# Attention front of a fused kernel: scale in the cast, negated maxima, constants made on chip, new order

## The chip, the cores and the metric

The kernel runs on one core of one Trainium2 chip. The metric is device time in microseconds (us), the median of several runs; lower is better. A core has a matrix engine (PE, with its weight loads shown as PEld), a vector engine (DVE), a scalar engine (ACT), a general engine (POOL), and a queue that issues DMAs (SP). ACT and POOL can issue DMAs too. Engines run their own instruction lists in order and wait for each other by semaphores.

## What is computed

Windowed attention with four sink tokens, then a feed-forward layer with a sigmoid-gated unit.

```python
def _attn_ref(q, k, v, n_sink, window):     # q, k, v: (4, 8, 768, 64)
    scale = 1.0 / np.sqrt(D)
    scores = scale * np.matmul(q, k.transpose(0, 1, 3, 2))
    keep = is_sink | in_window              # first 4 keys, or the last 128
    scores = np.where(keep, scores, -1000000000.0)
    scores = scores - np.max(scores, axis=-1, keepdims=True)
    a = np.exp(scores)
    a = a / (np.sum(a, axis=-1, keepdims=True) + 1e-09)
    return np.matmul(a, v).astype(np.float32)

def _moe_ref(x, w_in, w_out):               # x: (3072, 512), d_ff 2048
    h = x @ w_in
    g = h * (1.0 / (1.0 + np.exp(-1.702 * h)))
    return (g @ w_out).astype(np.float32)
```

## The kernel before

**Tiling.** The 4 x 768 rows are 24 blocks of 128 queries. Blocks 0, 6, 12, 18 are the first of each batch: they see only their own 128 keys. Every other block sees its own keys, the block's before it, and the four sinks. The first four are done first, then the rest in order (`BLOCKS`). The feed-forward works on groups of blocks: 0, 6, then 12 and 18 together, then pairs.

**One block, by the names of its operations** (b is the block; _0 and _1 are halves of four heads):

- `q`b, `k`b, `v`b: loads with a cast to 16 bits, issued by POOL. `wi0..3`, `wo0..3`: quarters of w_in and w_out, also by POOL.
- `tq`, `tk` and `cq`, `ck`: transposes of queries and keys on PE for the first blocks, and the copy out of PSUM (ACT or DVE). Later blocks use a DMA transpose (`tqk`, SP).
- `msk` (first blocks only): the causal mask is added into the scores by a matmul of an identity (`identb`) with a table (`bias0`). `sc`: the scores.
- `ks`b: sink keys of a batch packed into `ksb` (zeroed by `zk`), by two small copies. `snk`: sink scores. `ms`: their maximum. In block 1 it adds `bias1`, a 4-column mask.
- `pk`: copies masked scores in place, by the table `later`. `mx`: row maximum. First blocks: `nb` (maximum times -scale), then `bx`, the exponential with scale and that bias. Other blocks: `sb`, `ssb` (subtract), then `ex`, `exs`.
- `ta`, `ca` (PE transpose, copy) or `tat` (DMA transpose): probabilities transposed. `sp`, `so`: POOL cuts them into the previous block's part and the own part.
- `av`: probabilities times values, with the sinks' values from `vsb`. `nm`: normalization. `tx`, `cx` or `txd`: the result transposed.
- `h`g_u: first feed-forward product of group g. `th` and `g`: the gate. `o`b_n: second product. `ev`, `st`: copy out of PSUM and store.

**Sink values.** `zs` sets `vsa` to one, `vsa0..3` load four value rows of each batch into it (SP), and `vsb0..3` multiply that by the table `own` into `vsb`.

**Constants.** Six tables lie in the program and are loaded: `ident`, `identb`, `later`, `bias0` (32 KB each), `own` (32.5 KB) and `bias1` (1 KB). `za0..3`, `zv`, `z1`, `zk`, `zs` are memsets on DVE.

**Order.** All operations are listed in a plan, and a written list (`ORDER`, lines 55 to 89) names them by number in the order in which they are emitted; a letter picks the engine where there is a choice (d DVE, a ACT, p POOL, s SP). Each engine executes its own in that order. PSUM has three buffers `mm` for transposes and feed-forward products, two `sc`, one `av`; a new use waits until an older user has let its buffer go.

The front, decoded, engine by engine (before):

```
PE   tq0 msk0 tk0 sc0 tk18 tq12 tk6 tk2 ta0_0 tq6 msk6 ta0_1 tk12 av0_0 sc6 tk1 av0_1 tq1 tq18 tx0 snk1 ta6_0
     h0_1 av6_0 ta6_1 msk12 sc12 av6_1 h0_3 tx6 h0_2 h1_3 h1_2 msk18 h1_1 sc18 h0_0 ta12_0 h1_0 ta12_1 av12_0 o0_0
     ta18_0 av12_1 o0_1 sc1 tx12 o6_0 av18_0 tq2 o6_1 snk2 ta18_1 o6_2 o0_2 ta1_1 av18_1 o6_3 sc2 tx18 ta1_0 o0_3
     tk4 tq4 tk3 tq3 h2_2 ...
DVE  zs zk zv za1 z1 ck0 mx0_0 za0 vsb0 nb0_0 mx0_1 vsb2 nb0_1 ck6 vsb1 ks0 ck2 za2 ks6 za3 nm0_0 mx6_0 mx6_1 ...
ACT  ident own identb bias0 cq0 ck18 bx0_0 cq12 bx0_1 cq6 ca0_0 ca0_1 ck12 ck1 cq1 bx6_0 cx0 bx6_1 cq18 th0_1 ...
POOL q0 k0 k18 q12 k6 k2 q6 vsb3 v0 k12 v6 q18 k1 q1 wi1 wi3 wi2 v12 wi0 wo0 wo1 q2 v18 wo2 wo3 k3 q4 k4 q3 q5 v2
     v1 k5 sp1_1 v7 k7 sp1_0 so1_0 so1_1 v5 v4 k8 v3 q7 sp2_0 so2_0 q8 sp2_1 so2_1 ...
SP   vsa3 vsa1 vsa0 later vsa2 bias1 st0_ tqk5 tat3 tqk7 ...
```

Of the kernel before, what the change touches and what calls it, by code (L numbers as in the profile page):

```python
# [11 lines left out]
FP32 = mybir.dt.float32  # L12
FP16 = mybir.dt.float16
# [27 lines left out]
LH = 1.0  # L41
HW = set()
LD4 = 0.65
LD, LW, QKX, ATX, XTX, STX, SPX2 = 0.97, 2.55, 1.55, 1.56, 0.77, 0.85, 1.9
AHEAD = 4
TQ = set(BLOCKS[:8])
# [5 lines left out]
RING = dict(RING,qkn=7)  # L52


ORDER = """
1a 9 6 8d 100 15 4a 5a 11 14 7 96 0a 23 94 21 3s 98 17 2s 29 18 104 107 105a 101p 102 103d 16 108 171 20 109 150 19
172a 10 95d 125 110 24 112 225 111 99d 26 151a 113 126d 27 114 115 97d 88 127 106 128a 130 92 226d 116a 117 12 90 129
148 118a 119 13 131 149a 22 120 194 132 121 86 196 195a 135 173 197a 87 133 122 134 89 123 199 124a 200 138 30 136 613
139d 137 25 152 142 174a 140 143 153 614 141d 615 154 91 144 155 619 156 145 157 158 146 616 93 620 147d 159 160 621
637 32 617 634 638 618 176 639 635 631 36 175 636 177 632 610 178 633 161 611 181 35 628 162a 179 612 180 163 182 165  # L60
622 164d 166 629 184 183 33 167 623 185d 168 39 198 630 169 31 204 640 170a 205 188 227 189 641 228a 201 28 230 186
206 642 231 209 202 624 187a 203 215 190 38 643 208 191 207 229 216d 210 644a 192 217 235 211 43 193a 625 232 212a 236
41 280 282 626a 256 281d 258 213 283a 627 233 652 259a 214 237 257a 649 653 218 238 234 261 661 241 40 650 262 654 239
285 37 260 651 662 242 286 304 44 655 266 243a 263 34 219 656 646 663 42 657 658 647 244 220 664 648 659 245 267 670
45 665 660 240 221 671 264 268 246 672 247a 269 265 248 667 222 270 249 666 250 284 668 271 251 48 676 669 46 290 252
323 673 47 253 287 677 291 254 306 272 678 288 255a 674a 223 292 679 273 224a 293 289 682 680d 294 51 307 305 683 50
688 295 308 311 49 686 309 675 52 684 687 312 689 692 310 685 313 276 693 690 314 277 296 315 704 297 344 324 345 705
327 691 316 53 330 325 694 326 361 331 274 695 696 275 328 698 697 681 332 278 317 699 279a 333 329 298 334 318 343
299 700 346 54 347 300 706 55 349 335 701 57 301 350 302 645 319 303a 707 348 702a 352 351 716 708a 320 353 362 336
321 717 354 720 322 337 365 724 709 59 721 363 399 714 364 368 60 712 715 703 369 725 722 366 713 340 355 723 710 341  # L70
367 718 711 356 371 370 338 719 732 64 339 372 726 342 56 733 62 382 381 373 61 383 727 387 384 359 734 360 385 728
388 401 735 390 386 729 374 419 389 750 402 391 375 730d 400 736d 751 748 392 67 406 403 742 66 404 752 65 743 407 749
740 63 753 378 738 379 408 376 739 744 377 393 409 357 405 745 746 358 741 394 420 380 747 439 58 410 754 440 423 421
760 422 426 397 755 427 411 398 761 424 457 756 425 762 428 757 429 430 412 766 758d 438 759 413 767 763 431 444 69
441 770 737 442 71 768 771 445 72 764a 772 769 446 68 416 443 773 780 432 447 417 788 781 433 448 414 774 415 73 458
459 789 775 460 449 464 395 778 396 461 776 418 779 465 782 777 462 436 495 450 783 463 466 790 75 765 437 731 784 467
74 468 434 451 785 435 476 791 482 786d 800 792a 479 454 793 801 798 469 455 794 514 452 795 802 453 808 803 456 477
804 809 478 470 799 483 796 480 471 806 797 485 805 484 816 76 481 810 77 486 474 80 496 475 817 70 502 807 499 487
497 82 811 498 78 500 818 503 81 516 822 504 819 823 505 517 501 812 820a 506 515 821 824 488 518 813 489 825 507 828
814d 83 472 826 552 473 79 519 832 827 521 829 535 836 833 536 522 492 837 834 508 523 830 524 493 509 520 844 831 84  # L80
835 490 534 525 491 845 540 494 541 838 537 846 526 542 839 538 512 787 847 513 543 840 539 544 553 852 848a 545 527
573 864 853 574 590 528 510 841 511 865 559 860 842d 529 546 861 556 862 530 850 547 554 854 851 555 85 560 531 855
856 532 557 858 533 857 561 866 859 558 550 815 562 591 563 551 872 597 867 863 592 564 873 593 598 868 843 594 548
849 880 595 869 596 881 600 565 888 599 549 874 889 870d 566 601 886 875 884 876a 602 567 885 572 568 878 877 575 569
879 892 570 578 882 571 893 603 576 887 890 579 604 894 891 577 883 900 580 581 895 582 901 607 912 608 583 896 913
605 871 897 606 902 898a 910 584 916 911 585 914 917 918 915 908 919 906 909 586 907 903 587 922 588 920 589 923 609
921 904a 928 924 929 925 930 926d 946 931 947 934 942 935 932a 948 943 933 940 905 927 936 941 899 938 937 949 944 939
956 945 950 957 951 958 952 962 953 963 954a 959 964 955 960d 965 961 966d 967
# [48 lines left out]
def _consts():  # L137
    j = np.arange(P)[None, :]
    p = np.arange(P)[:, None]
    later = j > p  # L140
    bias0 = np.where(later & (j >= 4), NEG, 0.0).astype(ml_dtypes.bfloat16)
    bias1 = np.where(later[:, :4], NEG, 0.0).astype(ml_dtypes.bfloat16)
# [3 lines left out]
    return (  # L146
        np.eye(P, dtype=np.float16),
        later.astype(np.uint16),
        bias0,
        bias1,  # L150
        own.reshape(32, 8 * D1),
    )
# [3 lines left out]
def kernel(  # L156
# [20 lines left out]
    ident_np, later_np, bias0_np, bias1_np, own_np = _consts()  # L177
    ident_d = nc.inline_tensor(ident_np, name="cident")
    identb_d = nc.inline_tensor(ident_np.astype(ml_dtypes.bfloat16), name="cidentb")
    later_d = nc.inline_tensor(later_np, name="clater")  # L180
    bias0_d = nc.inline_tensor(bias0_np, name="cbias0")
    bias1_d = nc.inline_tensor(bias1_np, name="cbias1")
# [37 lines left out]
    o_bias0 = cdma("bias0", bias0, bias0_d.ap(), -1000)  # L220
    o_ident = cdma("ident", ident, ident_d.ap(), -999)
    o_bias1 = cdma("bias1", bias1, bias1_d.ap(), -998)
    o_later = cdma("later", later, later_d.ap(), -997)
    o_own = cdma("own", ownm, own_d.ap(), -996)
    o_identb = cdma("identb", identb, identb_d.ap(), -999.5)
# [111 lines left out]
    for bb in range(Bsz):  # L337
        o = plan.add(
            f"vsa{bb}", SP, 0.75, lambda bb=bb: nc.sync.dma_start(vsa[:, bb, 0:D], v[bb, :, 0:4, :]),
            deps=[z_s], dma=("v", 0.3), key=-500 + bb,  # L340
        )

        def vs_build(e, bb=bb):
            (nc.vector if e == DVE else nc.gpsimd).tensor_tensor(
                out=vsb[0:32, bb].rearrange("p l (j d) -> p (l j) d", d=D1),
                in0=vsa[:, bb].unsqueeze(1).to_broadcast((32, 8, D1)),
                in1=ownm.rearrange("p (n d) -> p n d", d=D1),
                op=ALU.mult,
            )

        o_vsb.append(plan.add(f"vsb{bb}", {DVE: 0.6, POOL: 1.15}, 0, vs_build, deps=[o, o_own, z_v], key=20))
# [12 lines left out]
    for pos, b in enumerate(BLOCKS):  # L364
# [5 lines left out]
        qkb = qkT[:, SLOT[b]]  # L370


        buf, n, unit = tunit[b]
        if b in OCT:
            parts = []
            before = used_slot.pop(SLOT[b], [])
            for w in (1, 0):
                tp = ps("mm", (P, 8, 4, 16), FP32, f"t{'qk'[w]}{b}")

                def t_qk(w=w, buf=buf, n=n, tp=tp):  # L380
                    for t in range(8):
                        for l in range(2):
# [11 lines left out]
                        f"c{'qk'[w]}{b}", {DVE: 0.6, ACT: 0.5}, 0,  # L394
                        lambda e, w=w, tp=tp, qkb=qkb: copy(
                            e, qkb[:, 4 * w : 4 * w + 4].rearrange("p c (u t) -> p c u t", t=8),
                            tp().rearrange("p t c u -> p c u t"),
# [5 lines left out]
        elif b in TQ:  # L403
# [3 lines left out]
            for w in (1, 0):  # L407

                def t_qk(w=w, buf=buf, n=n, tp=tp):
                    src = buf()[:, n, w].rearrange("p h d -> p (h d)")  # L410
                    for c in range(4):
# [9 lines left out]
                        lambda e, w=w, tp=tp, qkb=qkb: copy(e, qkb[:, 4 * w : 4 * w + 4], tp()[:, 4 * w : 4 * w + 4]),  # L421
# [19 lines left out]
        if r == 0:  # L441

            def sink_keys(bb=bb, qkb=qkb):
                for hl in range(2):
                    rows = slice(64 * hl, 64 * hl + 64)
                    nc.vector.tensor_copy(
                        out=ksb[rows, bb, :, 4 * hl : 4 * hl + 4], in_=qkb[rows, 4:8, 0:4]
                    )

            o_ks[bb] = plan.add(f"ks{b}", DVE, 0.45, sink_keys, deps=o_qkt[b] + [z_k], key=K0 - 10)  # L450
# [79 lines left out]
        for hf in range(2):  # L530
# [12 lines left out]
            def rowmax(hf=hf, t=sc[hf], own=own, small=small, ms=ms):  # L543
                part = small[:, 4 * hf : 4 * hf + 4].rearrange("p (j l) -> p l j", l=2)
                nc.vector.tensor_reduce(out=part, in_=t()[:, :, :, own], axis=AX.X, op=ALU.max)  # L545
# [353 lines left out]
```

## Time and profile before

| | |
|---|---|
| median of 3 runs | 233.18 us (233.18 to 233.24) |
| the profiled execution | 232.43 us, of which the span of instructions 230.7 us |
| granted PE clock | 1.00 |
| PE busy | 217.0 us, 94% of the span, 2202 matmuls |
| DVE busy | 154.5 us, 67% |
| ACT busy | 139.8 us, 61% |
| POOL busy | 111.2 us, 48% |
| moved by DMA | 32.07 MB, mean 139 GB/s |
| loads of q, k, v | 24 each, 128 KB as written, median 5.4 to 5.7 us from issue to landing |
| w_in, w_out | 4 loads each, 512 KB, median 10.4 and 15.4 us |

The span runs from the first to the last instruction; the profiled execution's own time has 1.7 us around it. In the profile an engine's line gives its busy share in forty equal slices, in tenths. The timeline lists instructions with their start and length in us and, in brackets, how long the engine had been idle before and what it had waited for. Matmuls are pipelined, so a busy PE can hide short stalls. A landing time is the issue's start plus the time to landing.

### The profile page before, as it was taken

Reading aid. Unit: us, or ns where it says so; the run is one execution under the profiler, and the core shown is the slowest. Engines: PE = TensorE matmul, PEld = TensorE weight load, DVE = VectorE, ACT = ScalarE, POOL = GpSimd, SP = SyncE. Lnnn points to the kernel's source line nnn. Section 1 sums busy time; section 2 is a strip of 40 time slices with the busy share of each in tenths; the row PEclk is TensorE's granted clock in tenths of the full one; section 3 lists DMA queues with packets and bytes.
Section 4 is the critical chain, followed back from the end, with each engine's and each line's share of the span. In section 5 each row is a group of like instructions: output and inputs, shape, how many; then the busy total and the mean of one; then the engine's idle time right before and its main releaser. Section 6 shows DMA issues by size and latency. Waiting matters only on the chain. (4 is left out here: it accounts for less than half of the span.)

```text
span 230.7 us, 5431 instructions
## 1 busy us (share of the span) xinstructions
PE 217.0 (94%) x2202; PEld 151.6 (66%) x2202; DVE 154.5 (67%) x388; ACT 139.8 (61%) x220; POOL 111.2 (48%) x129
## 2 busy tenths in 40 slices
PE   0878899999999999999999999999999999999994
PEld 0666865876586686486577496486686686775863
DVE  2487899999979976987797848668577847121001
ACT  2278774874597687168378386786358486631531
POOL 8983435995393869077392619265350312300000
PEclk9999999999999999999999999999999999999999
DMA  5999999999999899999999989999647542402312
GB/s 76 167 189 200 206 198 180 168 134 91 153 182 168 159 242 131 148 162 135 165 196 136 196 172 131 131 185 110 140 92 114 142 99 45 99 0 45 114 71 91
DMA packets 120904, 32.07 MB, mean 139 GB/s; under 512 B 112016, under 2 KB 117936, under 8 KB 120880
## 3 DMA queue, kind: packets, MB, share of 16 engines
q0 software_dynamic: 69888, 13.64, 72.2%
q1 hardware_dynamic: 50512, 17.96, 38.7%
q8 instruction: 17, 0.28, 0.5%
q10 hardware_dynamic: 480, 0.13, 0.3%
q14 instruction: 7, 0.06, 0.1%
HBM read 27.46 MB, written 6.29 MB: 146 GB/s over the span
## 5 line engine op out<-in xcount | busy, mean ns | idle before, releaser
L786 PE MATMUL hT<-xT,w_in 128*128 128x256 f16 (+1 forms) x832 | 93.2, 264 | 1.5 <-ACT gT L816 0.5
L836 PE MATMUL o<-w_out,gT 128*128 128x512 f16 (+2 forms) x400 | 92.1, 371 | 0.0
L786 PEld LDWEIGHTS <-w_in 128*128 128x128 f16 x832 | 73.9, 98 | 14.1 <-issue 3.7
L816 ACT ACTIVATE gT<-hT 128x512 f16<-128x512 f32 x80 | 45.8, 597 | 33.1 <-PE hT L786 32.9
L836 PEld LDWEIGHTS <-gT 128*128 128x128 f16 x400 | 36.1, 98 | 33.3 <-issue 1.9
L637 POOL TENSOR_SCALAR_AFFINE_SELECT atp<-at 128x1024 f16<-128x1024 f16 (+1 forms) x22 | 22.3, 1015 | 72.9 <-DMA at<-a 69.9
L545 DVE TENSOR_REDUCE mx<-sc 128x4 f32<-128x512 f32 x48 | 32.7, 683 | 0.8 <-PE sc L478 0.5
L606 ACT ACTIVATE a<-e 128x1056 f16<-128x1056 f32 (+2 forms) x24 | 22.5, 938 | 15.4 <-issue 12.5
L535 DVE COPY_PREDICATED sc<-later,sc 128x512 f32<-128x512 uint16 x40 | 26.8, 689 | 3.6 <-PE sc L483 3.3
L582 DVE TENSOR_TENSOR e<-sc,mx 128x512 f32<-128x512 f32 x40 | 26.7, 684 | 0.7
L722 DVE RECIPROCAL rcp<-av 128x4 f32<-128x4 f32 x48 | 8.6, 179 | 24.0 <-PE av L712 22.1
L637 POOL TENSOR_SCALAR_AFFINE_SELECT at<-at 128x1024 f16<-128x1024 f16 (+1 forms) x22 | 22.2, 1009 | 1.4
L271 POOL DMA_DIRECT2D v<-in_v_dram x24 | 21.7, 906 | 2.0 <-DMA w_in<-in_moe_w_in_dram 1.2
L723 DVE TENSOR_TENSOR xn<-av,rcp 128x256 f16<-128x256 f32 x48 | 20.4, 424 | 1.7
L241 DVE COPY osb<-o 128x512 f32<-128x512 f32 (+2 forms) x10 | 6.3, 634 | 21.2 <-PE o L836 21.1
L606 ACT ACT_TABLE_LOAD x12 | 15.4, 1283 | 6.1 <-DVE e L596 4.0
L318 POOL DMA_DIRECT2D qkn<-in_q_dram x18 | 16.1, 897 | 4.5 <-DMA w_out<-in_moe_w_out_dram 1.6
L816 ACT ACT_TABLE_LOAD x13 | 16.7, 1283 | 2.4 <-PE hT L786 1.8
L318 POOL DMA_DIRECT2D qkn<-in_k_dram x18 | 16.0, 890 | 3.6 <-DMA w_out<-in_moe_w_out_dram 3.4
L710 PE MATMUL av<-v,at 128*128 128x65 f16 x192 | 17.5, 195 | 0.1
L710 PEld LDWEIGHTS <-at 128*128 128x128 f16 x192 | 14.4, 98 | 2.7 <-DVE at L241 0.3
L712 PE MATMUL av<-v,atp 128*128 128x65 f16 x160 | 15.1, 194 | 0.0
(58 smaller groups left out, 198.1 us busy)
## 6 DMA issues: line engine op xcount, KB each, us to landing
out_dram<-osb SPq DMA_DIRECT2D x23, 256.0 KB, 3.2
qkn<-in_q_dram POOLq DMA_DIRECT2D x24, 128.0 KB, 5.7
qkn<-in_k_dram POOLq DMA_DIRECT2D x24, 128.0 KB, 5.4
v<-in_v_dram POOLq DMA_DIRECT2D x24, 128.0 KB, 5.5
w_in<-in_moe_w_in_dram POOLq DMA_DIRECT2D x4, 512.0 KB, 10.4
w_out<-in_moe_w_out_dram POOLq DMA_DIRECT2D x4, 512.0 KB, 15.4
at<-a SPq DMA_TRANSPOSE x18, 3.7
qkT<-qkn SPq DMA_TRANSPOSE x10, 4.3
```

The lines of the kernel that those rows point to most:

```text
L271: f"v{b}", POOL, 0.88, lambda b=b, view=view: nc.gpsimd.dma_start(v65[:, b, :, 0:D], view),
L318: lambda buf=buf, n=n, w=w, view=view: nc.gpsimd.dma_start(buf()[:, n, "qk".index(w)], view),
L535: nc.vector.copy_predicated(out=t()[:, :, :, own].rearrange("p l j s -> p (l j) s"), mask=later.unsqueeze(1).to_broadcast((P, 4, P)), data ...
L545: nc.vector.tensor_reduce(out=part, in_=t()[:, :, :, own], axis=AX.X, op=ALU.max)
L582: nc.vector.tensor_tensor(out=e32()[:, 512 * hf : 512 * hf + 512].rearrange("p (l j s) -> p l j s", l=2, j=2), in0=t()[:, :, :, own], in1= ...
L606: nc.scalar.activation(out=a16()[:, lo:hi], in_=e32()[:, lo:hi], func=AF.Exp, scale=scale)
L637: nc.gpsimd.affine_select(out=dst, in_=at()[:, lo : lo + num], pattern=[[0, num], [1 if own else -1, P]], compare_op=ALU.is_ge if own else ...
L710: nc.tensor.matmul(av()[:, i], at()[:, c], v65[:, b, h], start=(r == 0), stop=(r == 0))
L723: nc.vector.tensor_tensor(out=xn()[:, xi, 4 * hf : 4 * hf + 4].rearrange("p (j l) d -> p l j d", l=2), in0=av()[:, :, 0:D].rearrange("p (l ...
L786: nc.tensor.matmul(ht()[:, n].rearrange("p (n t) -> p n t", n=NT), w_in16[:, c, bass.ts(f, P)], t0()[:, i0 : i0 + NT, c], start=(c == 0), ...
L816: lambda fs=fs, gt=gt, ht=ht: nc.scalar.activation(out=gt()[:, fs[0] : fs[-1] + 1], in_=ht(), func=AF.Gelu_apprx_sigmoid),
L836: nc.tensor.matmul(po()[:, 0:width], gt()[:, F, bass.ts(t, P)], w_out16[:, F, c0 : c0 + width], start=(F == 0), stop=(F == NF - 1),)
```

## The change

1. **Scale.** For the four first blocks the queries are multiplied by the scale in the copy out of PSUM (`cq`), the maximum is written negated, and the exponential takes it as its bias with scale 1. The eight `nb` operations are gone.
2. **Constants.** `identb`, `bias0` and `bias1` are no longer loaded. DVE casts `identb` from `ident` and makes the masks from `later`: a multiply by -1e30, a copy of four columns, a memset of four columns. `later` and `ident` are issued by ACT, `own` by SP.
3. **Sink values.** `zs`, and with it the loads `vsa0..3`, come after the copy of the keys of block 2 (`ck2`); all four `vsb` run on DVE. `ks0`, `ks6` and `ks12` go to POOL.
4. **Order.** The whole list is written anew, with numbers shifted by the operations that are gone. Some copies change engine: `cq12`, `ck1`, `ca0_0`, `ca0_1` go from ACT to DVE, `ca12_1` from DVE to ACT; of the output copies `ev16`, `ev19`, `ev21` go to DVE, `ev3`, `ev4`, `ev20`, `ev23` to ACT.

```diff
+    o_identb = plan.add("identb", DVE, 0.12, lambda: nc.vector.tensor_copy(out=identb, in_=ident), deps=[o_ident], key=-900)
+
+    def masks():
+        nc.vector.tensor_scalar(out=bias0, in0=later, scalar1=NEG, scalar2=None, op0=ALU.mult)
+        nc.vector.tensor_copy(out=bias1, in_=bias0[:, 0:4])
+        nc.vector.memset(bias0[:, 0:4], 0.0)
+
+    o_bias0 = o_bias1 = plan.add("bias0", DVE, 0.35, masks, deps=[o_later], key=-900)
...
-        o_vsb.append(plan.add(f"vsb{bb}", {DVE: 0.6, POOL: 1.15}, 0, vs_build, deps=[o, o_own, z_v], key=20))
+        o_vsb.append(plan.add(f"vsb{bb}", DVE, 0.62, vs_build, deps=[o, o_own, z_v], key=20))
...
+        prescaled = NEGATE and b in NB
+        qf = [scale if prescaled else 1.0, 1.0]
...
-                            tp().rearrange("p t c u -> p c u t"),
+                            tp().rearrange("p t c u -> p c u t"), qf[w],
...
-            o_ks[bb] = plan.add(f"ks{b}", DVE, 0.45, sink_keys, deps=o_qkt[b] + [z_k], key=K0 - 10)
+            o_ks[bb] = plan.add(f"ks{b}", {DVE: 0.45, POOL: 0.6}, 0, sink_keys, deps=o_qkt[b] + [z_k], key=K0 - 10)
...
+                if neg:
+                    nc.vector.tensor_reduce(out=part, in_=t()[:, :, :, own], axis=AX.X, op=ALU.max, negate=True)
+                    return
...
-                o = plan.add(f"nb{b}_{hf}", DVE, 0.09, neg, deps=[o], key=K0 - 29)
-
-                def bexp(hf=hf, t=sc[hf], own=own, a16=a16, nbias=nbias):
+                if not prescaled:
+                    o = plan.add(f"nb{b}_{hf}", DVE, 0.09, neg, deps=[o], key=K0 - 29)
+
+                def bexp(hf=hf, t=sc[hf], own=own, a16=a16, nbias=nbias, scale=1.0 if prescaled else scale):
```

The front, decoded (after):

```
PE   msk0 tq0 tk0 tq12 tq6 sc0 tk1 tk6 tk2 ta0_0 msk6 sc6 tq1 tk12 av0_0 ta0_1 tk18 snk1 ta6_0 av0_1 ta6_1 msk12
     tx0 tq18 av6_0 sc12 h0_1 av6_1 tx6 h0_3 h1_3 msk18 h0_2 h1_2 h1_1 h0_0 sc18 ta12_0 h1_0 ta12_1 av12_0 o0_0
     av12_1 ta18_0 o0_1 sc1 av18_0 tx12 o6_0 tq2 o6_1 snk2 ta18_1 o0_2 o6_2 ta1_1 av18_1 o6_3 sc2 ta1_0 tx18 o0_3
     tk4 tq4 tq3 tk3 h2_2 ...
DVE  za3 za0 bias0 identb za1 za2 zv z1 ck0 cq12 mx0_0 zk mx0_1 ck1 ck6 ca0_0 ck2 zs mx6_0 mx6_1 nm0_0 ca0_1 ms1
     ca6_0 nm0_1 ca6_1 vsb3 vsb0 nm6_0 mx12_0 nm6_1 mx12_1 cx6 ks18 ...
ACT  later ident cq0 cq6 bx0_0 bx0_1 cq1 bx6_0 bx6_1 ck18 ck12 cx0 cq18 bx12_0 th0_1 ...
POOL k0 q0 q12 q6 q1 k1 k6 k2 k12 k18 v0 wi1 ks0 v6 q18 wi3 wi2 wi0 wo0 v12 wo1 v18 q2 wo2 wo3 q3 ks12 q4 k4 k3 v7
     v5 v3 v1 sp1_1 k5 sp1_0 so1_0 q5 ks6 v2 q7 k7 so1_1 v8 sp2_0 q8 v4 k8 so2_0 sp2_1 so2_1 ...
SP   own vsa3 vsa0 vsa1 vsa2 tqk5 tat3 tqk7 ...
```

More of the change, by code (lines that the diff above doesn't have):

```diff
@@ L41 @@
 LH = 1.0
+OCTDT = "FP32"
 HW = set()
@@ L45 @@
 AHEAD = 4
+AVT = set()
+NEGATE = False
 TQ = set(BLOCKS[:8])
@@ L52 @@
 RING = dict(RING,qkn=7)
+NEGATE = True
 ORDER = """
[L56 to L64, printed above, removed]
@@ L89 @@
+918 937 926 922 938 933 923d 931 924 934 862 939 896 932 927 929 928 940 941 930 935 942 936 947 943 948 953 944 949
+945a 954 950 946 955 951a 956 952 957d 958
 """
@@ L140, in _consts @@
     later = j > p
-    bias0 = np.where(later & (j >= 4), NEG, 0.0).astype(ml_dtypes.bfloat16)
-    bias1 = np.where(later[:, :4], NEG, 0.0).astype(ml_dtypes.bfloat16)
     own = np.zeros((32, 2, 2, 2, D1), np.float16)
@@ L148, in _consts @@
         later.astype(np.uint16),
-        bias0,
-        bias1,
         own.reshape(32, 8 * D1),
@@ L341, with vs_build @@
         )
-        def vs_build(e, bb=bb):
-            (nc.vector if e == DVE else nc.gpsimd).tensor_tensor(
+        def vs_build(bb=bb):
+            nc.vector.tensor_tensor(
                 out=vsb[0:32, bb].rearrange("p l (j d) -> p (l j) d", d=D1),
@@ L393 @@
                     plan.add(
-                        f"c{'qk'[w]}{b}", {DVE: 0.6, ACT: 0.5}, 0,
-                        lambda e, w=w, tp=tp, qkb=qkb: copy(
+                        f"c{'qk'[w]}{b}", {DVE: 0.65 if OCTDT == "FP32" else 0.38, ACT: 0.5}, 0,
+                        lambda e, w=w, tp=tp, qkb=qkb, qf=qf: copy(
                             e, qkb[:, 4 * w : 4 * w + 4].rearrange("p c (u t) -> p c u t", t=8),
-                            tp().rearrange("p t c u -> p c u t"),
+                            tp().rearrange("p t c u -> p c u t"), qf[w],
                         ),
@@ L420 @@
                         f"c{'qk'[w]}{b}", {DVE: 0.36, ACT: 0.49}, 0,
-                        lambda e, w=w, tp=tp, qkb=qkb: copy(e, qkb[:, 4 * w : 4 * w + 4], tp()[:, 4 * w : 4 * w + 4]),
+                        lambda e, w=w, tp=tp, qkb=qkb, qf=qf: copy(
+                            e, qkb[:, 4 * w : 4 * w + 4], tp()[:, 4 * w : 4 * w + 4], qf[w]
+                        ),
                         deps=[a] + before, give=[tp], key=K0 - 40,
@@ L553 @@
                 if nbias is None:
-                    nbias = const.tile([P, 8], FP32, name=f"nb{b}")
+                    nbias = small if prescaled else const.tile([P, 8], FP32, name=f"nb{b}")
                 def neg(hf=hf, nbias=nbias, small=small):
```

71 lines of the change are left out of this document (36 added, 35 removed).

## The prediction

> **What bounds the kernel now.** I read the page's 40 slices first, then the chain of waits, then the timeline of the first 62 us, and last, for single transfers, the time from issue to landing.
>
> ```profile
> PE   0878899999999999999999999999999999999994
> ...
> DVE  2487899999979976987797848668577847121001
> ...
> POOL 8983435995393869077392619265350312300000
> ...
> DMA  5999999999999899999999989999647542402312
> ...
> PE 35%; ACT 2%; issue 1%; DVE 0%
> ```
>
> A slice is 5.77 us. PE is full from about 24 us (fifth slice) to the end; DMA is full from the second slice to about 160 us. The chain is almost all PE. In windows, PE is busy 15.61 of the first 25 us (9.4 us idle), and from there to 225 us it is idle only 1.3 us. So two things can move the end: when PE's steady stretch begins, and how much it stalls inside it.
>
> ```profile
> 24.04 0.74 POOL L331 DMA_DIRECT2D w_out<-in_moe_w_out_dram  x1 [1.79 <-DMA w_in<-in_moe_w_in_dram]
> ...
> 32.51 0.87 POOL L318 DMA_DIRECT2D qkn<-in_q_dram  x1 [1.64 <-DMA w_out<-in_moe_w_out_dram]
> ...
> 39.49 1.02 PE L836 MATMUL o<-w_out,gT 128*128 128x512 f16 x4
> ...
> 42.37 1.12 PE L412 MATMUL tq<-ident,qkn 128*128 128x128 f16 x16
> ...
> 43.33 1.93 PE L786 MATMUL hT<-xT,w_in 128*128 128x256 f16 x16
> ```
>
> (start, length, engine, instruction, idle before it and what ended it.) The steady stretch begins on the heels of the loads. The last quarter of w_out (`wo3`) is issued at 24.04 and lands 15.4 us later, at 39.4; PE uses it at 39.49. `wo2` lands at 21.50+15.4=36.9, used at 37.29. Keys of block 4 land at 30.01+12.1=42.1, used at 42.37. Queries of block 3 land at 32.51+10.5=43.0; their four transposes are the last of the sixteen at 42.37, 56 ns apart, so they begin at 42.37+12x0.056=43.05. Slack 0.05 to 0.4 us: up to `h2_2` (43.27), where the groups of two blocks begin, **the stream of loads is as late as PE**. POOL can't issue sooner either: each load from the 20th on starts 0.2 to 0.3 us after the eighth before it has landed (wo3 after wi2's 12.5+11.3=23.8; q3 after wo1's 16.29+15.9=32.2). In windows of 4 us the DMA share is 1.23 to 1.54 and 162 to 208 GB/s from 10 to 38 us, never a hole.
>
> **The change, part by part.**
>
> *Scaling in the cast, negated maxima.* Eight `nb` operations leave DVE (0.15 to 0.36 us each, some 1.6 us by the rows at L557). The scale rides in the cast of the first queries, which keeps its row (ACT 0.58, DVE 0.69). The maximum keeps its 0.68. In front of the first exponential:
>
> ```profile
> 9.40 0.69 DVE L545 TENSOR_REDUCE mx<-sc 128x4 f32<-128x512 f32 x1 [0.49 <-PE sc L478]
> ...
> 10.05 0.11 DVE L231 MEMSET a<- 128x64 uint32 x1
> 10.08 0.62 DVE L344 TENSOR_TENSOR vsb<-vsa,ownm 32x520 f16<-32x520 f32 x1
> ...
> 10.64 0.36 DVE L557 TENSOR_SCALAR nb<-mx 128x4 f32<-128x4 f32 x1
> ...
> 11.03 1.14 ACT L568 ACTIVATE a<-sc,nb 128x128 f16<-128x128 f32 x4 [0.26 <-DVE nb L557]
> ```
>
> The maximum is ready at 10.09 and the exponential starts at 11.03: 0.94 us of which all but about 0.1 goes.
>
> *Order of the front, walked by hand.* The first ten loads are q and k. By position: first pair 5.6 and 6.2, then 0.84 us a load (10.65 for the seventh before): q6 8.15, k1 9.6, k6 10.65, k2 11.5, k18 13.2. `tq0` 6.2, `tk0` 6.65, `tq12` 7.35, `tq6` 8.2, `sc0` 8.65, first maximum 9.2 to 9.9, exponentials 9.85 to 12.1 (11.03 to 13.69 before). `ta0_0` stands behind `tk2` and so behind k2: 11.9 (12.70 before). `msk6` 12.4, `sc6` 13.2, `av0_0` 14.6, `ta0_1` 14.8, `tk18` 15.2, `bx6` 15.0 to 17.3, `tx0` 18.1, `cx0` to 19.15, `h0_1` 19.3 against 20.04. Four operations that followed `h0_1` before (`ta6_1`, `msk12`, `av6_0`, `sc12`: 0.39+0.60+0.29+0.40 by their rows, 1.4 us in sequence) are done by then. PE's lead: 0.7+1.4, **about 2 us**. It then meets the loads: `h0_2` needs wi2 (23.8 before; PE used it at 24.35), `o0_1` needs wo1 (32.2; used at 32.91), `o6_3` needs wo3. Up to wo3, and again up to the 28th load, both orders hold the same loads. What of the lead survives at `h2_2` is what the stream itself gains.
>
> *Constants.* bias0, identb (32 KB each) and bias1 (1 KB, in 8-byte packets) are not loaded; `later` (32 KB) moves from SP at 3.61 to the head of ACT's queue at 0.8, where DMA has room (26 to 75 GB/s between 2 and 3.5 us against 136 to 201 after 4). That takes 97 KB out of the full stretch. At 181 GB/s (window 6 to 10) this is 0.54 us; I take **0.55**. Bounds: 0.73 at the 134 GB/s of 3 to 6 us; 0 if those packets only filled gaps.
>
> By the Trainium skill, page DMA: Bandwidth & Descriptors, section "Why small descriptors are slow", a 256-byte descriptor carries 27% overhead on an engine. The removed tables have rows of 256 bytes, so by that page the term would be an estimated 0.70 us. The trace has no row that separates it.
>
> *Added on DVE:* the masks (a multiply over 128x128, a 4-column copy, a memset) and the cast of identb. No row has them; between a 0.11 us memset and a 0.42 us 128x512 copy each, 0.4 to 1.7 us for four. They wait for `later` and ident, which land by about 3.2 (ownm, issued second at 1.18 before, took 2.0), and DVE has nothing to cast before 6.8: free. Without that cover `msk0` would hold PE at most 1 us, inside the 2 us lead.
>
> *Sink values.* `zs` now stands after `ck2` (13.5), and four SP issues (0.7 each, L339) wait for it. `vsb3` is next on DVE at about 17.5; a landing of 2 to 4.4 us gives 15.7 to 18.1, so at most 0.6 us of DVE, with `nm6_0` and `mx12_0` behind it: again inside the lead. All four builds now run on DVE (0.62 to 0.68), ks0, ks6, ks12 on POOL (unknown: 0.34 to 0.78 on DVE, up to 1.2 by the POOL row at L344). `ks0` waits on POOL for `zk` (about 10.0) with `v6`, `q18` and w_in behind it; with six loads in flight then (five of 128 KB, one of 512), 6 us at 181 GB/s, DMA does not run dry.
>
> *After 43 us.* PE's set and nearly its order are the same; at `h2_2` all 66 earlier operations are the same ones. DVE is nearly full from 40 to 60 (19.23 of 20 us) and gets `sc1` about 1 us sooner (wo1 31.7, `o0_1` 0.9), without `ca12_1`. PE's one wait for it there ("hT <-DVE gT", 0.15 at 47.42) should go: 0.15, bounds 0 and the 0.7 us by which 43.27 to 61.56 exceeds its matmuls (8 `h` at 0.87, 8 `o` at 0.863, 2 `sc` at 0.54, 4 `av` at 0.35, some 1.3 of transposes and sinks: 17.6 of 18.3).
>
> **Sum:** 0.55 (constants) + 0.05 (slack at q3) + 0.15 = 0.75 us. Span 230.7 to 229.95, the profiled run 232.43 to 231.7; the median, 0.75 above that run, 233.18 to **232.4**.
>
> **Rivals.**
> *A, the lead goes through.* If loads follow PE rather than bound it, 2 us come off: 231.2. For it: PE idles 9.4 us in front. Against: slacks of 0.05 to 0.4 us at five loads in a row.
> *B, no lead in the stream.* The constants ride in gaps, or the first loads are issued later. Time 233.1. For it: total GB/s is 201 while the constants flow (5.0 to 5.5) and 189 just after (6.0 to 6.5). By the Trainium skill, page SBUF — State Buffer, section "Who interferes with whom", a DVE copy or multiply in a two-port mode locks GpSimd out for its whole length. The new masks and cast fall among POOL's first ten issues; POOL's row there that ran beside a DVE memset took 0.78, the others 0.60 to 0.66, so four such holds would cost up to about 0.5 us, which is the whole term: B's time again.
> *C, slower: POOL's new order between 40 and 54 us.* Before, `sp2_0` and `so2_0` ran at 49.44 to 50.8. Now q5, ks6, v2, q7, k7 stand ahead of `so1_1`, and q8, v4, k8 (0.9 each) between `sp2_0` and `so2_0`. From `sp1_0` at 42.2: so1_0 43.5, q5 44.4, ks6 45.0, v2 45.9, q7, k7 47.7, so1_1 48.3, v8 49.2, sp2_0 49.9, three loads 52.6, so2_0 53.2. `av2_0` now comes right after `o12_2`, at 53.9; v2 lands at 45.0+6 to 8=51 to 53. Slack 0.7. It decides once POOL slips by more: a ks6 of 1.2 and one 0.9 us wait for a landing put so2_0 at 54.7 and, with 0.4 to start, PE 1.2 us late, with no room to make it up; without the 0.15, that is 232.4+1.2+0.15=233.8. Against: POOL's waits at loads end as the backlog shrinks (issue to landing 15.4, 10.5, 5.9 us).
>
> **How the numbers follow.** Forecast 0.45 (232.0 to 232.7), A 0.13, B 0.23, C 0.19. 0.2% is 0.47 us, about what a measurement of this kernel tells from no change: faster is below 232.7, slower above 233.65. Faster: A and the forecast, 0.58; same: B, 0.23; slower: C, 0.19. The range runs from A to just above C, 231.2 to 233.9.
>
> **What would show it.** Right: `h0_1` near 19.3 but `h2_2` near 42.6; wo3 landing at about 38.9 with PE's second stage starting on it; new PE waits ended by w_in, w_out; L557 gone. Wrong: `h2_2` at 41.3 (A), wo3 at 39.4 (B), a PE wait before `av` ended by POOL `at` or DMA v near 54 us (C), or new stalls beyond 62 us, where I compared only orders.

## The result, and the profile after

The changed kernel is slower. Its median is 235.53 us over 22 runs (232.59 to 236.86), that of the kernel before 233.09 us over 22 runs beside it (231.9 to 235.42); the ratio is 1.0072, 95% interval 1.0044 to 1.01. The forecast was 232.4 us and the range ended at 233.9. The first three runs of the kernel before agreed within 0.06 us and hid how far both kernels spread; that 0.2% could be told from no change was too fine, since even 22 runs a side leave 0.3% on either side. The ratios, here and below, leave out runs more than 1.5% above the fastest of their kernel, which the medians and ranges hold; the profiled runs of the changed kernel (236.15), e1, e3 and e6 are such long ones.

The profiled run took 236.15 us, its span 234.4. The page's slices of PE and its chain of waits, changed kernel:

```profile
PE   1696989999999989999999999999889999999994
...
PE 66%; DMA 19%; DVE 8%; POOL 3%; issue 2%; ACT 1%; POOLq 0%; SPq 0%; DVEq 0%; ACTq 0%
```

A slice is 5.86 us. PE's row now has an 8 in slices 15, 29 and 30 (82 to 88 us, 164 to 176 us), where before there were only nines. The chain now runs through DMA for a fifth of the span. That can't be set against the chain of the kernel before, whose shares add up to 38%: it was followed back only to 140.6 us. Of the 19% here, some 12 are the loads of the first 33 us (one each of q, w_in and w_out: 5.6, 7.7 and 15.7 us); 6 are two transposes, of 7.5 and 7.0 us, the second at 162 us, where the chain before has none. The windows view says where PE stands still (us; busy time with number of instructions; clock, DMA share, GB/s). Before:

```profile
0.00:25.00 25.00, 15.62 (x300) 12.37 (x301) 15.35 (x45) 13.32 (x34) 18.30 (x29) 1.00 1.19 162
...
80.00:92.00 12.00, 12.00 (x127) 9.26 (x126) 8.60 (x22) 9.69 (x14) 9.15 (x10) 1.00 1.53 188
...
160.00:176.00 16.00, 16.00 (x157) 11.31 (x157) 11.30 (x31) 8.60 (x12) 5.19 (x5) 1.00 0.75 118
```

After:

```profile
0.00:25.00 25.00, 15.60 (x304) 12.34 (x305) 16.00 (x44) 11.89 (x33) 16.70 (x29) 1.00 1.15 161
...
80.00:92.00 12.00, 10.91 (x120) 8.61 (x119) 9.21 (x22) 7.92 (x14) 5.76 (x6) 1.00 1.51 163
...
160.00:176.00 16.00, 14.18 (x130) 9.11 (x128) 10.50 (x27) 7.07 (x10) 5.93 (x7) 1.00 1.25 128
```

PE (first pair of numbers after the length) gained nothing in the first 25 us, and it lost 1.1 us between 80 and 92 and 1.8 us between 160 and 176. The clock is 1.00 in both.

**The front.** Timeline of the changed kernel (start, length, engine, instruction, idle before it and what ended it):

```profile
9.78 0.69 DVE L552 TENSOR_REDUCE mx<-sc 128x4 f32<-128x512 f32 x1
10.50 1.65 ACT L578 ACTIVATE a<-sc,mx 128x128 f16<-128x128 f32 x6 [0.45 <-DVE mx L552]
14.05 3.06 SPq L341 DMA_DIRECT2D vsa<-in_v_dram  x4
19.64 0.69 DVE L346 TENSOR_TENSOR vsb<-vsa,ownm 32x520 f16<-32x520 f32 x1 [1.40 <-DMA vsa<-in_v_dram]
19.80 0.44 PE L387 MATMUL tq<-ident,qkn 128*64 128x64 f16 x16 [1.37 <-DMA qkn<-in_q_dram]
20.69 0.69 DVE L346 TENSOR_TENSOR vsb<-vsa,ownm 32x520 f16<-32x520 f32 x1 [0.36 <-DMA vsa<-in_v_dram]
20.74 0.73 PE L796 MATMUL hT<-xT,w_in 128*128 128x128 f16 x10
21.98 0.29 PE L720 MATMUL av<-v,at 128*128 128x65 f16 x4 [0.18 <-DVE xn L733]
```

The maximum ends at 10.47 and the exponential starts at 10.50: the 0.94 us in front of it are gone. Two waits eat the lead. `tq18` waits 1.37 us for its queries, which POOL now issues at 11.85 behind `wi1` and which land at 19.76 (before: 9.19 and 14.11); that puts `h0_1` at 20.74, where it was 20.04. And the sink values, issued from 14.05 on, reach DVE only at 19.6 and 20.7: DVE stands still for 1.76 us in all, and `nm6_0` and the next maximum are queued behind the builds. In this profile PE was late itself and lost only 0.18 us by that, at `av6_1` (21.98). In another profile of the same kernel (e1 below) the queries came 1.1 us earlier, and the sink values took what that left:

```profile
22.48 0.30 PE L720 MATMUL av<-v,at 128*128 128x65 f16 x4 [1.61 <-DVE xn L733]
```

**Behind 80 us.** The chain of the changed kernel at both places where PE stalls (start, length, what):

```profile
78.45 7.53 DMA at<-a
...
86.11 1.10 POOL atp L647
...
87.26 1.10 POOL at L647
...
162.49 7.02 DMA at<-a
...
169.63 1.09 POOL atp L647
170.72 0.83 POOL v L273
...
171.56 1.12 POOL at L647
```

Waits of PE there (what waited, on what, us in total, times, longest), from 80 to 92 us:

```profile
PE av L720 <- POOL at L647: 1.1, 1, 1.1
```

and from 160 to 176 us:

```profile
PE hT L796 <- DMA xT<-xn: 1.0, 1, 1.0
...
PE av L720 <- POOL at L647: 0.8, 1, 0.8
```

A transpose of the probabilities takes 7.0 to 7.5 us, POOL cuts it up, and PE waits for the cut, at 88.41 and 172.73. At the second place a transposed result (`xT`) is late too and takes 1.0 of the 1.8 us; had it been in time, PE would have stood that much longer at `av`. The kernel before, the same two transposes in its timeline:

```profile
77.08 0.89 POOL L318 DMA_DIRECT2D qkn<-in_q_dram  x1
77.20 1.34 SPq L681 DMA_TRANSPOSE at<-a  x1
...
82.71 1.09 POOL L637 TENSOR_SCALAR_AFFINE_SELECT atp<-at 128x1024 f16<-128x1024 f16 x1 [2.99 <-DMA at<-a]
...
158.27 0.90 POOL L318 DMA_DIRECT2D qkn<-in_q_dram  x1
161.16 1.29 SPq L681 DMA_TRANSPOSE at<-a  x1
...
164.50 1.08 POOL L637 TENSOR_SCALAR_AFFINE_SELECT atp<-at 128x1024 f16<-128x1024 f16 x1 [5.34 <-DMA at<-a]
```

There they took at most 5.5 and 3.3 us. Ahead of the first, the kernel before has one load; two more follow behind it. In the changed kernel POOL issues loads at 77.00 and 77.87 ahead of the first, and at 161.20 and 162.08 ahead of the second. The page has a median landing of 6.1 us for `at<-a` against 3.7 before, but the trace holds the landing of only 8 and 9 of the 18, and not of the same blocks. For the four blocks in both, it went from 6.0 to 3.4 us (block 3), 4.8 to 6.7 (4), 3.3 to 7.9 (10) and 7.5 to 10.3 (16). By the Trainium skill, page DMA: Bandwidth & Descriptors, section "Issuing engines are not separate DMA queues", transfers issued by different engines run on the same DMA engines and interleave; these transposes, issued by SP right among POOL's loads, agree with that.

Start of named PE operations in one profile of each kernel (us), for this and the next section:

| | before | after | e2 | e4 | e5 | e9 | e10 | e11 | e12 | e15 | e16 |
|---|---|---|---|---|---|---|---|---|---|---|---|
| h0_1 | 20.04 | 20.74 | 19.98 | 18.91 | 18.59 | 18.52 | 18.41 | 18.55 | 18.81 | 20.46 | 21.01 |
| o6_3 | 39.49 | 39.91 | 39.31 | 37.95 | 38.01 | 37.94 | 37.91 | 37.95 | 37.89 | 40.30 | 41.95 |
| h2_2 | 43.33 | 43.70 | 43.40 | 42.38 | 42.26 | 42.23 | 42.04 | 42.15 | 42.08 | 44.09 | 45.75 |
| h4_3 | 80.08 | 80.20 | 80.31 | 78.78 | 80.19 | 78.88 | 80.10 | 78.84 | 78.05 | 80.51 | 82.22 |
| av7_0 | 88.57 | 90.41 | 88.80 | 88.74 | 88.68 | 89.70 | 88.85 | 87.82 | 87.13 | 89.53 | 91.66 |
| o14_3 | 163.09 | 164.16 | 163.18 | 163.65 | 163.28 | 163.82 | 162.55 | 161.47 | 161.93 | 163.33 | 165.88 |
| h9_2 | 171.61 | 174.83 | 171.70 | 172.83 | 171.80 | 172.34 | 171.51 | 171.78 | 170.45 | 171.85 | 174.40 |
| o23_13 | 227.16 | 230.73 | 227.25 | 228.85 | 227.35 | 227.89 | 227.48 | 227.72 | 225.99 | 227.40 | 229.95 |

### The profile page after: what moved, and what is told of

Read it like the earlier page. It is cut to its first block, busy times and chain, and to the rows that moved or that the text cites. A ratio compares the mean times of both kernels' runs of the same rounds, so it can differ in the third digit from the quotient of the medians.

```text
span 234.4 us, 5429 instructions
## 1 busy us (share of the span) xinstructions
PE 217.8 (93%) x2202; PEld 151.0 (64%) x2202; DVE 155.5 (66%) x381; ACT 138.7 (59%) x218; POOL 110.8 (47%) x134
## 4 chain that ended last, share of the span: by engine, by line
PE 66%; DMA 19%; DVE 8%; POOL 3%; issue 2%; ACT 1%; POOLq 0%; SPq 0%; DVEq 0%; ACTq 0%
PE o L846 28%; PE hT L796 27%; DMA w_out<-in_moe_w_out_dram 7%; DMA at<-a 6%; PE sc L489 3%; DMA w_in<-in_moe_w_in_dram 3%; DMA qkn<-in_q_dram 2%; PE av L720 2%; DVE mx L554 2%; PE av L722 2%; PE av L715 1%; DVE mx L557 1%; DVE xn L733 1%; DVE e L592 1%; POOL at L647 1%
## 5 line engine op out<-in xcount | busy, mean ns | idle before, releaser
L554 DVE TENSOR_REDUCE mx<-sc 128x4 f32<-128x512 f32 x40 | 27.3, 682 | 0.2
L243 DVE COPY osb<-o 128x512 f32<-128x512 f32 (+1 forms) x9 | 5.9, 651 | 28.3 <-PE o L846 21.0
L247 ACT COPY osb<-o 128x512 f32<-128x512 f32 (+1 forms) x12 | 6.7, 572 | 14.5 <-PE o L846 14.5
## 6 DMA issues: line engine op xcount, KB each, us to landing
w_in<-in_moe_w_in_dram POOLq DMA_DIRECT2D x4, 512.0 KB, 10.8
```

## The experiments

Each ratio is of some 9 to 12 runs to 23 to 35 runs of the kernel before on the same chip.

**Front or tail (e1 to e3).** Up to `h2_2` both orders hold the same operations of PE, so they can be crossed there.

```diff
 e1: the changed kernel
 e2: the changed kernel's code, and its order up to h2_2
-order from h2_2 on of the changed kernel
+order from h2_2 on of the kernel before (ks6 on DVE)
 e3: the kernel before, with its order up to h2_2
-order from h2_2 on of the kernel before
+order from h2_2 on of the changed kernel
```

> The changed kernel once more, on the chip of the next three. Tail theory (the loss comes from the order after h2_2, where POOL's loads stand behind selects that wait for DMA transposes) and front theory (it comes from the front: sink values loaded late, DVE held, constants) both expect 0.5 to 1.5% above the kernel before.

> The changed kernel, but everything that its order emits from h2_2 on is emitted in the sequence and on the engines of the kernel before. Tail theory: within 0.3% of the kernel before (232.5 to 233.8), with the 0.4 us at h2_2 still there. Front theory: as slow as the changed kernel, 234.3 to 236.

> The kernel before up to h2_2, and from there the sequence and engines of the changed kernel. Tail theory: 0.5 to 1.5% slower than the kernel before. Front theory: within 0.3% of it.

Measured: e1 235.18 us, ratio 1.0045 (1.001 to 1.0081); e2 232.78, 0.999 (0.9957 to 1.0023); e3 235.3, 1.0075 (1.004 to 1.011). With the new order behind `h2_2` the kernel is slower with either kernel's front (e1, e3); with the old one it is level (e2, whose interval is clear of the 22 runs' 1.0044 to 1.01). The new front by itself is worth nothing that shows.

**The sink values early (e4, e5).** In ORDER of the changed kernel 8 is `zs`, and 99, 93, 95, 97 are `vsa3`, `vsa0`, `vsa1`, `vsa2`:

```diff
 e4
-1a 12 2s 9 13 0a 14 20 4
+8 1a 12 2s 99 93 95 97 9 13 0a 14 20 4
...
-89 187 8 129 99 143 85 188a 131 116 114 93 130 86
-164 117 95 115d 190 21 132 191 133 97 118
+89 187 129 143 85 188a 131 116 114 130 86
+164 117 115d 190 21 132 191 133 118
 e5: e4 up to h2_2
-order from h2_2 on of the changed kernel
+order from h2_2 on of the kernel before
```

> The changed kernel with zs first on DVE and the four sink-value loads at the head of SP's queue, as before; nothing else is moved. DVE should no longer wait 1.8 us before the vsb builds, and h0_1 should start at 19.3 to 19.9 instead of 20.7. Front theory: 1 us or more faster than the changed kernel. Tail theory: at most 0.4 us, since wo3 lands at 39.4 either way.

> The front of e4 (new front, sink values loaded at once) and from h2_2 on the sequence and engines of the kernel before. If the front's gain and the tail's loss are two separate things: h2_2 near 42.4 instead of 43.3, nothing lost behind, 0.2 to 0.6% faster than the kernel before (231.6 to 232.5). If the front's gain is always given back behind h2_2: within 0.2% of it.

Measured: e4 233.96 us, 1.0003 (0.9963 to 1.0043); e5 232.64, 0.9972 (0.9944 to 1.0001). By the medians e4 is 1.2 us faster than e1, as its front theory had it, but the intervals overlap. In both profiles, the front is 1.0 us ahead of the kernel before at `h2_2`. e5 gives that back by `h4_3`, and its interval takes in both of its cases; waits of PE between 45 and 75 us in e5 (what waited, on what, us in total, times, longest):

```profile
PE snk L513 <- DVE ss L526: 1.0, 1, 1.0
```

DVE is nearly full there (busy 19.53 of the 20 us from 40 to 60), so PE's lead ends at it. In e4 the new order carries the lead as far as `h4_3` (1.3 us, of which 0.35 is `av5_0`, which this order does only behind `h4_3`), and loses it, and more, behind 80 us.

**POOL's order (e6, e7).** POOL's list behind `h2_2` is put into the other order's sequence, every other engine's kept.

```diff
 e6: e4
-POOL's list behind h2_2 as in the changed kernel
+POOL's list behind h2_2 as in the kernel before
 e7: e5
-POOL's list behind h2_2 as in the kernel before
+POOL's list behind h2_2 as in the changed kernel
```

> e4, but POOL's operations behind h2_2 (loads and selects) are in the sequence of the kernel before; PE, DVE, ACT and SP keep the changed order. POOL theory (loads queued behind selects, selects behind loads): most of the tail's loss goes, 231.6 to 232.8. Other-engines theory (PE's or DVE's order asks for values too soon): stays at e4's 233.4 to 234.5.

> e5, but POOL's operations behind h2_2 are in the changed sequence. POOL theory: slower than e5 by 1 us or more. Other-engines theory: within 0.5 us of e5.

Measured: e6 234.61 us, 1.0027 (0.9993 to 1.0062); e7 235.32, 1.0065 (1.0034 to 1.0095). POOL's old list doesn't mend the new order, and its new list costs the old order 0.9% (e7 against e5): the engines' lists fit together, and a mismatch costs by itself. So the whole list of an engine was too big a piece to swap.

**The constants loaded again (e8).**

```diff
 e8: e5
-identb cast on DVE from ident; bias0 and bias1 made on DVE from later
+identb and bias0 loaded by ACT's queue, bias1 by SP's, at the same places in the order
```

> e5, but identb, bias0 and bias1 are loaded again (two issues on ACT behind ident, one on SP behind own) instead of made on DVE. If their 65 KB cost the stream of loads 0.35 us (two thirds of the predicted 0.55), wo3 lands that much later and the time is 0.1 to 0.2% above e5; if they ride in gaps, no difference.

Measured: 233.49 us, 0.9995 (0.9967 to 1.0024). 0.85 us above e5, with overlapping intervals: the sign was as forecast, the size open (e15 below). In its profile `wo3` lands at 40.36, against 37.96 in e5.

**Where to switch, and POOL's loads (e9 to e11).**

```diff
 e9: e4 up to h4_3
-order from h4_3 on of the changed kernel
+order from h4_3 on of the kernel before
 e10: e5 up to h4_3
-order from h4_3 on of the kernel before
+order from h4_3 on of the changed kernel
 e11: e4, POOL's list alone
-so1_0 q5 ks6 v2 q7 k7 so1_1 v8 sp2_0 q8 v4 k8 so2_0 sp2_1 so2_1 sp3 q9 so3 q10 k10 k9 sp4 v10 v9 so4
+so1_0 ks6 q5 v2 k7 so1_1 v4 k8 q7 sp2_0 so2_0 q8 sp2_1 so2_1 q9 v8 k9 sp3 so3 q10 k10 v9 v10 sp4 so4
```

> Order of e4 (changed kernel with the sink values' loads early) up to h4_3, then before's order. Theory (the front's gain is real, the new order keeps it to 80 us, and all of the loss is behind 80 us): h4_3 near 78.8 in the profile, 1.2 to 1.4 us ahead of before, and from there to o23_13 the 147.1 us that before takes; about 231.7 us, ratio 0.994 to 0.996. Rival (a stretch of the old order behind the switch gives the lead back, as e5 did behind 43 us, because the order sets what every engine finds ready): level with before by 90 us, 232.6 to 233.1, ratio 0.997 to 1.0.

> Order of e5 up to h4_3 (early front, before's order from h2_2 to h4_3), then the changed kernel's order. Theory (the loss is in the new order behind 80 us, whatever went ahead): h4_3 near 80.2, then 1.5 to 3.5 us more than before from there to the end; 234.0 to 236.0 us, ratio 1.004 to 1.012. Rival (the loss comes from where the stretch of 43 to 80 us leaves the buffers and loads, so that the later order is sound by itself): 232.6 to 233.2, ratio 0.997 to 1.0.

> e4 with one thing changed: between h2_2 and av7_0, POOL's loads (q7, q8, v8, k9, v9, v10 and a few neighbours) stand against its selects as they do in before, most of them earlier; every other queue as in e4. Theory (the stall of 80 to 90 us comes from these loads, which stand behind sp3 and so3 in the new order and then run into the transposes tat4 and tat7): h4_3 to av7_0 in 8.9 to 9.1 us instead of e4's 9.96, the stretches behind as in e4; about 1 us faster than e4, 232.8 to 233.2. Rival (the runs' own spread of the transfers makes the stall): 9.7 to 10.2 us in that stretch again and 233.8 to 234.2.

Measured: e9 233.2 us, 0.9985 (0.9954 to 1.0017); e10 233.93, 1.0011 (0.998 to 1.0043); e11 233.49, 1.0024 (0.9991 to 1.0056).

e9 is its rival's case: at `h4_3` it is 1.2 us ahead, and 10.8 us later, at `av7_0`, 1.1 us behind. Its chain there:

```profile
76.77 8.27 DMA at<-a
...
85.17 1.10 POOL atp L647
```

Again a transpose that goes out among POOL's loads (three from 75.32 to 77.95). The loads stood where the new order has them, so the stall came although the rest was old. PE itself stood mostly for another transpose, that of the queries and keys of block 9, and reached the `av` of block 7 so late that 0.2 us was left to wait for there; from 78 to 92 us:

```profile
PE sc L489 <- DMA qkT<-qkn: 1.8, 1, 1.8
PE av L720 <- POOL at L647: 0.2, 1, 0.2
```

e10 lies between its two theories, and its profile took from `h4_3` to the end only 0.3 us more than before: the new order stalls in some runs and not in others.

e11 did in its profile what the theory said: from `h4_3` to `av7_0` it takes 8.98 us (9.96 in e4; 8.49 before, without `av5_0`, which makes 0.35 of the difference). The other profiles agree. Where `v11` and `q11` are issued 1.5 and 0.6 us ahead of the transpose of block 7 (changed kernel, e1, e3, e4, e9), POOL starts to cut it 7.0 to 8.4 us after its issue, and the stretch takes 9.5 to 10.8 us; where they stand behind it (e11 to e16), it is 3.4 to 5.0 and 9.0 to 9.7 us. It is 1.6 us ahead of the kernel before as far as `o14_3`; then, at the second place, it loses 1.8 and is 0.2 behind at `h9_2`. Its time doesn't show the 1 us: its ratio is above that of e4, and the two intervals lie over each other.

**The second place (e12 to e14).** What was open here, and what each run was to tell, is in the expectations.

```diff
 e12: e11 up to o4_3
-order from o4_3 (93 us) on of the changed kernel
+order from o4_3 on of the kernel before
 e13: e11 up to o14_3
-order from o14_3 (161 us) on of the changed kernel
+order from o14_3 on of the kernel before
 e14: e11, POOL's list alone
-sp19 v23 so19
+sp19 so19 v23
```

> Order of e11 up to o4_3 (the front early, POOL's loads ahead of sp3 and so3), from there before's order. Theory (the lead is lost only where a transpose of the softmax is late and POOL's loads stand between its selects): o4_3 near 93.6, 1.7 us ahead of before, and from there the 131.9 us that before takes; span 229.0 to 229.6, 231.6 to 232.2 us, ratio 0.993 to 0.997. Rival (a switch of orders costs the lead wherever it is made, as in e9): level with before within 10 us of the switch, 232.8 to 233.4, ratio 0.998 to 1.002.

> Order of e11 up to o14_3, from there before's order (so without the new order's place at 163 to 172 us). Theory: o14_3 near 161.5, then before's 64.1 us to o23_13; span 229.0 to 229.6, 231.6 to 232.3 us, ratio 0.993 to 0.997. Rival (the new order between 92 and 160 us loses in most runs what one profile happened not to lose): 233.0 to 234.0 us, ratio 1.0 to 1.004, and more spread than e12.

> e11 with one instruction moved: POOL's load v23, which stands between the two selects sp19 and so19 (0.83 us of its queue, on the chain of waits), goes behind so19, where before has it behind so20. Theory (the place between the selects costs its issue time one for one): the stretch from o14_3 to h9_2 in 9.3 to 9.6 us instead of 10.3, 0.8 us faster than e11, ratio 0.997 to 1.0. Rival (the late transpose alone sets the stall): 9.9 to 10.6 us again, ratio 1.001 to 1.004 as e11.

Measured: **e12 231.77 us, 0.992 (0.9888 to 0.9951)**; e13 232.52, 0.9966 (0.9935 to 0.9998); e14 233.03, 0.9978 (0.9948 to 1.0008). e12 is faster than the kernel before and the changed one, and its nine runs lie within 231.06 and 232.74. Its interval is clear of those of e4 and e11, so the new order behind 93 us costs about 1%, shown in time and not only in a profile. A switch at 93 us loses little: from `o4_3` to `o23_13` e12 takes 132.1 us, before 131.9. The ratio of e13 is the one of its theory, but its interval overlaps those of e11 and e12.

In e14 the load is behind the selects and off the chain:

```profile
160.28 2.47 SPq L691 DMA_TRANSPOSE at<-a  x1
...
166.28 1.09 POOL L647 TENSOR_SCALAR_AFFINE_SELECT atp<-at 128x1024 f16<-128x1024 f16 x1 [5.57 <-DMA at<-a]
...
167.44 1.09 POOL L647 TENSOR_SCALAR_AFFINE_SELECT at<-at 128x1024 f16<-128x1024 f16 x1
168.48 0.89 POOL L273 DMA_DIRECT2D v<-in_v_dram  x1
```

The transpose is still late (6.0 us), but the second select follows the first, and PE no longer waits for POOL there, only 0.5 us for `xT`; the stretch from `o14_3` to `h9_2` is 9.20 us against 10.31 in e11 (8.52 before). That agrees with the theory. It isn't settled by it: e4 has the load between the selects and took 9.18 in its profile, and the intervals of e14 and e11 overlap.

**The front's two terms, on e12 (e15, e16).**

```diff
 e15: e12
-identb cast on DVE; bias0 and bias1 made on DVE
+identb and bias0 loaded by ACT's queue behind later and ident, bias1 by SP's
 e16: e12
-zs first on DVE, vsa3 vsa0 vsa1 vsa2 right behind own on SP
+zs behind ck2, the four loads behind it (the changed kernel's own order up to h2_2)
```

> e12 with identb, bias0 and bias1 loaded by DMA from the program's constants again (two issues on ACT's queue and one on SP's, at the places where e12 makes them on DVE). Theory of the prediction (the constants cost their share of the load stream, 0.55 us): h2_2 at 42.6 to 42.8, 232.2 to 232.6 us, 0.4 to 0.8 us slower than e12. Rival A (the load stream doesn't feel them): h2_2 as in e12, 231.6 to 232.0 us. Rival B (what e8's profile showed: they land late, the first scores wait for them, and the whole lead is gone): h0_1 behind 20, h2_2 behind 44, 233.2 us or more, ratio near 1.0.

> e12 with the changed kernel's own order up to h2_2, so with the sink values' loads behind the first keys and zs late, and everything from h2_2 on as in e12. Theory (DVE's wait for them costs the front's lead and nothing else binds there): h0_1 at 19.8 to 20.7, h2_2 at 43.3 to 43.8, 1.0 to 1.5 us slower than e12, 232.7 to 233.3 us, ratio 0.996 to 1.0. Rival (the loads bind the front, as the prediction had it, so that PE's wait at 20 us is made up by 38 us): o6_3 within 0.3 us of e12's 37.89, 231.7 to 232.1 us, ratio 0.991 to 0.994.

Measured: e15 232.61 us, 0.9989 (0.9967 to 1.0011); e16 233.48, 1.0024 (0.9996 to 1.0052). Both intervals are clear of e12's, which ran on another chip, with the kernel before beside it on each. In e15 PE's first wait tells the reason; waits of PE in the first 22 us, e15:

```profile
PE sc L475 <- DMA identb<-cidentb: 6.9, 1, 6.9
```

and e12:

```profile
PE sc L470 <- DVE identb L220: 3.7, 1, 3.7
```

`msk0`, first in PE's list, waits 3.2 us longer, so `tq0` comes later and `h0_1` starts at 20.46 instead of 18.81. That is rival B by its profile and its ratio (1.6 us above e12's; the medians, from two chips, differ by 0.84, close to the theory), and it prices the loads at these places of these queues, not the bytes alone.

In e16 the timeline has the changed kernel's wait again:

```profile
21.42 0.69 DVE L346 TENSOR_TENSOR vsb<-vsa,ownm 32x520 f16<-32x520 f32 x1 [1.48 <-DMA vsa<-in_v_dram]
```

`av6_1` waits 1.25 us for DVE behind it. The profile, of the longest of the twelve runs, overstates the price: the keys of block 2, issued at 5.51 in both, landed at 12.99 instead of 10.34, ahead of anything that differs. The runs, 1.0% slower than e12 by the ratios, carry the verdict: the late sink values cost what e12 had gained.

## Why the prediction was wrong, point by point

**Sink values: "again inside the lead" failed.** The landing was taken as 2 to 4.4 us. At 14 to 17 us the four loads go out into a full load stream: 5.6 us from the first issue to the first build, 1.4 to 1.8 us of DVE instead of at most 0.6. With them early (e4, e5, e12) `h0_1` starts at 18.6 to 18.9, better than the 19.3 of the forecast, and DVE doesn't wait for them. With them late (e16) the whole gain is gone in the runs.

**"DMA does not run dry" missed what stands behind `ks0`.** For `v6` and `q18`, now behind `ks0` and `wi1`, I asked only whether the queue stays full, and never walked `tq18`, which had some 3.5 us to spare before (landed at 14.11, used behind `tq1` at about 17.7). It has none now: 1.37 us of PE in the first profile, 0.39 in e12. How much of the runs' loss it makes wasn't tried by itself. The same place ties the loads to PE's front: `ks0`, now in POOL's queue, waits for `zk`, which DVE now does behind the first maximum. In the changed kernel `ks0` starts at 10.61, the loads behind it with it, and DMA moves 155 GB/s from 10 to 14 us; in e12 it starts at 9.49, and it is 189. In the profiles with `ks0` on POOL, `wo3` lands at 37.7 to 38.1 in the nine where `ks0` starts before 10.2, and at 38.2 to 40.4 in the seven where it starts later. What made the first maximum late differs (the masks in e8 and e15, else first loads that landed late, which may hold up the stream by themselves), and no run moved `ks0` or `zk` alone.

**Loads bound the front: right, once PE is ahead.** In e12 `wo3` lands at 37.83 and `o6_3` starts at 37.89 (in e4 37.91 and 37.95), and `h2_2` is 1.25 us ahead of before (0.95 and 1.07 in e4 and e5). With the sink values early this gain is more than the forecast's 0.55 + 0.05. In the changed kernel's profile `wo3` landed at 39.44, as before at 39.45, and none of the gain arrived.

**Constants, 0.55 us: the sign was right, the mechanism only in part.** e15 puts a higher price on them, 1.6 us by the ratios, and by its profile it comes in by the masks' landing, which holds PE's first transposes back, and with them `ks0` (11.28 in e8, 11.55 in e15) and the loads behind it. `wo3` lands 2 us later than in e12, and neither e8 nor e15 tells how much of that is bytes.

**Masks, identity cast and maxima: right.** The masks and the cast took 0.63 us on DVE between 2.68 and 3.50 us, `msk0` started at 3.55, and no later wait goes back to them. The rule that a DVE copy in a two-port mode locks POOL out, which the prediction put beside rival B (the Trainium skill, page SBUF — State Buffer, section "Who interferes with whom"), doesn't show: four loads issued by POOL from 2.08 on took 0.59 us each beside these four operations. The 0.78 us of POOL's first load, which the prediction read as such a hold, was 0.77 here with DVE idle from 1.08 to 2.68 us.

**"After 43 us. PE's set and nearly its order are the same" failed, and with a front that gains nothing it decided the sign (e2 level, e3 slower).** PE's set was indeed the same; the order of POOL's loads against its selects was not. I followed POOL as far as 54 us, for rival C. C did not occur at its place: `av2_0` started at 54.62, 0.7 us earlier than before, and PE's wait of 0.15 us at 47 us is gone, as forecast. The same kind of fault came behind 80 us, where the prediction "compared only orders": loads issued around a transpose that PE needs soon, and one load between its two selects. The kernel before had 1.5 us to spare between the cut of block 7 (`so7`, 83.86 to 84.96) and its first use, `av7_1` at 86.47; the new order had none (87.26 to 88.35, use at 88.41).

e2 and e3 show that the tail carries the loss, e12 against e11 that the part behind 93 us costs 1% with an unchanged front. That the loads' places are the cause is shown for e11's first place in profiles alone, not in time, and for `v23` it is likely. One more piece behind 93 us is in the table: from `h9_2` to `o23_13` the new order takes 55.9 to 56.0 us in all eight profiles that have it there, the old one 55.5 to 55.6 in the ten others, with the same operations of PE. Of these 0.4 us, 0.25 to 0.4 is `h10_4`, which starts 0.05 us after DVE has copied out block 15 (`ev15`) in each of the eight. What else behind 93 us costs time is open: e13 and e14 recover about half each by their ratios, with intervals that overlap that of e11, and e6 says that it isn't POOL's list alone.

**The chain.** "The chain is almost all PE" was read from shares that add up to 38%; they cover only the span behind 140.6 us and say nothing of what bounds the kernel ahead of it.

**The range.** It was built from cases within the first 62 us. Nothing in it stood for a tail that I had not walked.

## What to carry to other kernels

A transfer that is moved is priced at the load of the place it goes to, and with all that stands behind its consumer, not at its row from where it was. A lead made in front is worth only what the order behind can carry: here about 1 us was lost by the old order in the middle (e5) and by the new one behind 80 us (e4), and only the splice of both kept it (e12). When an order is written anew, the slack of every late transfer (landing to use) is to be read along the whole span, since a place with 1.5 us of slack and one with none look alike in a list. An operation that is put into the queue of loads ties them to whatever it waits for.

## What the runs showed of the hardware

How late a DMA transpose lands goes with the loads just ahead of it. The 18 traces hold the landing of 164 transposes of probabilities: the 112 with none of POOL's loads issued in the 1.5 us ahead of them took 3.2 to 6.9 us (median 3.4), the 28 with two took 5.7 to 10.3 (median 7.7). The issue itself was then longer on SP's queue at times (2.27 and 2.47 us against 1.29).

The transfers differ from run to run by more than the effects in question: the keys of block 2 landed at 10.34 and at 12.99 us from the same issue time, and the runs of one kernel spread over 1.7 us (nine of e12) to 5.5 us (twelve of e3). The kernels with the new order to the end (e1, e3, e4, e6, e10, e11, e14) spread over 3.9 to 5.5 us, those that end with the old order over 1.7 to 4.2, so a profile of one run can show a stall that the next run doesn't have; what holds are the intervals.
